# Attention block and gated MLP in one kernel: softmax scaling and weight split moved to ScalarE, local probabilities transposed by DMA from batch 2, block sums added from PSUM on VectorE

## The chip, the cores and the metric

The kernel runs on one core of a Trainium2 chip. The metric is the time of one execution on the device in microseconds (us). Engines are named as in the profile: PE is TensorE, DVE is VectorE, ACT is ScalarE, POOL is GpSimd, SP is the engine that issues the DMAs.

## The reference

q, k and v are 8 batches x 8 heads x 576 positions x 64. Each head runs two attentions and adds them: one over positions averaged in groups of 4 (144 of them), repeated back to 576, and one over a band of seven neighbours. The 4608 x 512 result goes through a gated MLP.

```python
q_d = q.reshape(B, H, Sd, factor, D).mean(axis=3)      # k_d, v_d alike; factor 4
out_up = np.repeat(sm_attn(q_d, k_d, v_d), factor, axis=2)
mask = np.abs(pos[:, None] - pos[None, :]) < factor
scores = np.where(mask, scale * np.matmul(q, k.transpose(0, 1, 3, 2)), -1000000000.0)
attn = np.exp(scores - np.max(scores, axis=-1, keepdims=True))
attn = attn / (np.sum(attn, axis=-1, keepdims=True) + 1e-09)
attn_out = out_up + np.matmul(attn, v)
x = attn_out.transpose(0, 2, 1, 3).reshape(B * S, H * D)
return (1.0 / (1.0 + np.exp(-(x @ w_gate)))) * (x @ w_val) @ w_out
```

## The kernel before

A unit is one pair of heads of one batch: 32 units, four a batch, unit u belongs to batch u // 4. For each unit the local attention works on 10 blocks of 58 queries against 64 keys, two heads on two halves of the partitions. Its steps are s0 and s1 (scores, tile `s`, 40 products of 64x64; scaled and masked into `t`, 128 x 640), then maximum, subtraction and exp on `t`, step sm (sum, reciprocal, multiplication), steps a0 and a1 (`t_local`: five 128x128 transposes by PE into PSUM, tile `at`, and the split of the result into two float16 parts), and step x (`av_local`: 30 products into tile `x`, to which DVE adds the pooled result `od`; then the split of the sum for the MLP). The pooled attention has the steps prep2 and vd (sums of 4 on POOL), d0 and d1 (products `sd`, exp with accumulated sums), dn (normalised into `ad`), at (`adt`, transposes by PE) and od.

float32 operands of the MLP are carried as two float16 parts (hi and lo) and multiplied with three products. The weights of gate (g) and value (v) are rebuilt from 64-bit words in batch 0 (`wjoin`), scaled by a power of two and split (`wsplit`, lines 280 to 296): DVE, ACT or POOL scales in place, ACT casts hi, POOL subtracts for lo.

Batches 0 and 1 run the MLP plainly: gate and value products (`pg`, `pv`), tanh on ACT, `act_val` on DVE, then the output products `po`. During batch 1, `sums` builds combinations of weight blocks and stores them to DRAM (`wd`). Batches 2 to 7 use seven products in place of eight for each pair of blocks (function `pair`, lines 804 to 873): six matmuls a product, and the seven results are added up by s1, s6, s7, s2, s5, s3 and s4 from five PSUM buffers (pool `ps_m`) into SBUF.

The work of the units of batch b + 1 is strewn over the MLP of batch b. The table `T` gives every step a position; all steps are sorted by it and emitted, and a scheduler then fixes one order of instructions on each engine, which each engine keeps at run time. An engine that waits for a semaphore holds up all that stands behind it in its order. SP issues every DMA in one such order.

Of the kernel before, what the change touches and what calls it, by code (L numbers as in the profile page):

```python
# [64 lines left out]
def attention_moe(ctx, tc, qk, qkd, v, vd, wg, wv, wo, mask, out):  # L65
# [214 lines left out]
    def wsplit(k, i):  # L280
# [126 lines left out]
    def sum4(out, x, eng=nc.gpsimd):  # L407

        nc.gpsimd.tensor_tensor(out=x[:, :, 0:2], in0=x[:, :, 0:2], in1=x[:, :, 2:4], op=ALU.add)  # L409
        for ps, o, g in out:  # L410
            eng.tensor_tensor(out=o, in0=x[ps, g, 0], in1=x[ps, g, 1], op=ALU.add)
# [24 lines left out]
    def unit_steps(u):  # L436
# [3 lines left out]
        plain = u < NPLAIN  # L440
# [27 lines left out]
        def prep2():  # L468
# [4 lines left out]
            sum4([(ALL, s["qd"], slice(0, SD))] + [(ps, s["kd"][ps, h], slice(SD, 2 * SD)) for h, ps in enumerate(HALVES)], x)  # L473

        def s_products(groups):
# [9 lines left out]
            if u < NPAIR:  # L485
# [602 lines left out]
```

## Time and profile before

| | us |
|---|---|
| median of 3 runs | 1049.86 (1049.4 to 1056.17) |
| the profiled execution | 1052.21 |
| its span, first to last instruction | 1050.4 |

| engine | busy us | share of the span |
|---|---|---|
| PE | 1017.0 | 97% |
| DVE | 752.5 | 72% |
| POOL | 537.2 | 51% |
| ACT | 475.0 | 45% |

The busy time of an engine is that of its instructions; of PE the ends are modelled, so that it reads as nearly full also where it waits a little. A share over the whole span hides that the stages have different limits: the start (weights and batch 0, up to about 175 us), batch 1 (to about 350 us), five alike batches of some 119 us, and the last batch, which has no attention beside it. The granted clock of PE is 1.00 in nearly every slice after 325 us.

### The profile page before, as it was taken

How to read it: one execution, taken by the hardware profiler on the slowest of the kernel's cores; microseconds unless marked ns; L12 is line 12 of the kernel's file. 1: busy time of each engine (PE TensorE's matmuls, PEld its weight loads, DVE VectorE, ACT ScalarE, POOL GpSimd, SP SyncE). 2: the span in 40 equal slices, each digit the busy share in tenths (PEclk: the TensorE clock that was granted, in tenths of full speed). 3: DMA queues.
4: the chain of work that ended last, by engine and by line, in shares of the span. 5: the costliest groups of instructions: out<-in, count | busy, mean ns of one | idle time of the engine just before them, and what ended most of it. 6: DMA issues, size and time to landing. Idle time of an engine off the chain costs nothing.

```text
span 1050.4 us, 23772 instructions
## 1 busy us (share of the span) xinstructions
PE 1017.0 (97%) x9587; PEld 813.0 (77%) x9587; DVE 752.5 (72%) x1417; ACT 475.0 (45%) x1064; POOL 537.2 (51%) x579
## 2 busy tenths in 40 slices
PE   8997989998989999999999999999999999999998
PEld 6875768876767887787778887787778887887776
DVE  6989989478796788747886479747886479825640
ACT  4868756334443444434443344524544344522320
POOL 7435378442554648545673548545573557512320
PEclk9999998999998999999999999999999999999999
DMA  9458943332434356344553356344563355313501
GB/s 366 158 177 254 352 146 130 130 123 99 145 141 152 127 202 228 118 148 164 200 206 117 127 197 251 122 147 141 192 234 102 132 190 192 117 35 119 179 31 46
DMA packets 53245, 169.01 MB, mean 161 GB/s; under 512 B 12560, under 2 KB 18832, under 8 KB 53136
## 3 DMA queue, kind: packets, MB, share of 16 engines
q1 hardware_dynamic: 53136, 167.50, 46.0%
q8 instruction: 75, 1.23, 0.5%
q14 instruction: 34, 0.28, 0.1%
HBM read 147.03 MB, written 20.45 MB: 159 GB/s over the span
## 4 chain that ended last, share of the span: by engine, by line
PE 65%; DVE 17%; ACT 6%; issue 5%; DMA 4%; POOL 2%; SPq 0%; DVEq 0%; POOLq 0%; ACTq 0%
PE po L420 27%; PE pv L420 14%; PE pg L420 14%; PE x L420 2%; PE s L483 2%; DVE vblk L192 2%; DVE tanh L719 2%; DVE arena L828 2%; PE sd L420 2%; PE od L420 2%; DMA v<-in_v_dram 1%; DMA wd<-arena 1%; ACT gq L865 1%; DVE arena L784 1%; PE at L580 1%
## 5 line engine op out<-in xcount | busy, mean ns | idle before, releaser
L420 PEld LDWEIGHTS <-arena 128*128 128x128 f16 x4176 | 407.0, 98 | 130.0 <-issue 16.1
L420 PE MATMUL po<-gq,wo 128*128 128x288 f16 x2304 | 295.2, 288 | 3.2 <-ACT gq L191 3.2
L420 PE MATMUL pg<-arena 128*128 128x288 f16 x2088 | 278.3, 287 | 6.1 <-DVE tanh L719 2.4
L420 PE MATMUL pv<-arena 128*128 128x288 f16 x2088 | 278.3, 288 | 6.0 <-DVE arena L828 2.7
L420 PEld LDWEIGHTS <-wo 128*128 128x128 f16 x2304 | 225.5, 98 | 61.5 <-issue 3.7
L828 POOL TENSOR_TENSOR arena<-arena 128x288 f32<-128x288 f32 x126 | 121.8, 971 | 122.7 <-ACT arena L842 92.2
L828 DVE TENSOR_TENSOR arena<-pv,arena 128x288 f32<-128x288 f32 x180 | 78.3, 447 | 50.4 <-PE pv L420 32.2
L746 DVE TENSOR_SCALAR arena<-po,osc 128x288 f32<-128x288 f32 x32 | 16.5, 515 | 82.9 <-PE po L420 82.8
L192 DVE SCALAR_TENSOR_TENSOR vblk<-v,svb,vblk 64x640 f16<-64x640 f32 x52 | 66.2, 1273 | 6.4 <-ACT vblk L191 4.4
L191 ACT ACTIVATE vblk<-v,svb 64x640 f16<-64x640 f32 x52 | 42.9, 825 | 44.5 <-PE x L420 24.9
L828 DVE TENSOR_TENSOR arena<-pg,arena 128x288 f32<-128x288 f32 x126 | 54.8, 449 | 5.0 <-PE pg L420 3.0
L514 POOL TENSOR_TENSOR t<-t,mx 128x640 f32<-128x640 f32 x32 | 44.3, 1384 | 26.6 <-DVE mx L513 15.2
L565 POOL TENSOR_TENSOR ad<-e,sme 72x288 f32<-72x288 f32 x54 | 42.1, 797 | 22.0 <-DVE sme L556 13.3
L524 POOL TENSOR_TENSOR t<-t,sm 128x640 f32<-128x640 f32 x24 | 35.5, 1479 | 29.2 <-DVE sm L522 21.1
L409 POOL TENSOR_TENSOR qkd<-qkd 128x576 f32<-128x576 f32 x29 | 36.7, 1265 | 26.1 <-DMA qkd<-in_qkd_dram 25.9
L548 ACT ACTIVATE e<-sd,mxd 72x144 f32<-72x144 f32 x128 | 47.0, 371 | 1.9 <-POOL ad L565 0.4
L409 POOL TENSOR_TENSOR vd<-vd 128x384 f32<-128x384 f32 x29 | 25.0, 862 | 43.5 <-DMA vd<-in_vd_dram 42.9
L420 PE MATMUL sd<-kdblk,qks 128*72 128x288 f32 x128 | 42.8, 416 | 3.8 <-ACT e L548 2.6
L775 POOL TENSOR_TENSOR arena<-arena 128x1024 f32<-128x1024 f16 x12 | 26.6, 2214 | 38.9 <-DMA wd<-arena 34.2
L295 POOL TENSOR_TENSOR arena<-arena 128x512 f16<-128x512 f32 x24 | 33.1, 1395 | 25.4 <-ACT arena L294 25.2
L483 PE MATMUL s<-qk 64*64 64x64 f32 x1200 | 43.3, 224 | 0.0
L483 PEld LDWEIGHTS s<-qk 64*64 64x64 f32 x1200 | 38.6, 137 | 6.0 <-issue 3.9
(147 smaller groups left out, 1543.8 us busy)
## 6 DMA issues: line engine op xcount, KB each, us to landing
arena<-wd SPq DMA_DIRECT2D x72, 896.0 KB, 4.6
qk<-in_qk_dram SPq DMA_DIRECT2D x30, 610.0 KB, 5.1
qkd<-in_qkd_dram SPq DMA_DIRECT2D x29, 576.0 KB, 3.9
vd<-in_vd_dram SPq DMA_DIRECT2D x29, 384.0 KB, 4.1
v<-in_v_dram SPq DMA_DIRECT2D x32, 320.0 KB, 4.5
arena<-in_wg_dram SPq DMA_DIRECT2D x12, 512.0 KB, 4.3
arena<-in_wv_dram SPq DMA_DIRECT2D x12, 512.0 KB, 4.5
arena<-in_wo_dram SPq DMA_DIRECT2D x12, 512.0 KB, 5.9
```

The lines of the kernel that those rows point to most:

```text
L191: nc.scalar.activation(hi, src, AF.Copy, scale=sc)
L192: return nc.vector.scalar_tensor_tensor(out=lo, in0=src, scalar=sc, in1=hi, op0=ALU.mult, op1=ALU.subtract)
L295: nc.gpsimd.tensor_tensor(out=lo, in0=a, in1=hi, op=ALU.subtract)
L409: nc.gpsimd.tensor_tensor(out=x[:, :, 0:2], in0=x[:, :, 0:2], in1=x[:, :, 2:4], op=ALU.add)
L420: nc.tensor.matmul(o, w[a], x[c], start=first and i == 0, stop=last and i == len(pairs) - 1)
L483: return nc.tensor.matmul(o, qkraw[u][ps, g * R : g * R + WIN], kw[ps, g], start=True, stop=True)
L514: nc.gpsimd.tensor_tensor(out=t, in0=t, in1=mx.unsqueeze(2).to_broadcast([P, NBLK, WIN]), op=ALU.subtract)
L524: eng.tensor_tensor(out=t, in0=t, in1=sm.unsqueeze(2).to_broadcast([P, NBLK, WIN]), op=ALU.mult)
L548: nc.scalar.activation(s["e"][:, qb, h, :], pt[:QM, h * SD : (h + 1) * SD], AF.Exp, bias=mx[:, h : h + 1], scale=QKSCALE / 16, accum_out=s ...
L565: eng.tensor_tensor(out=AD[:, qb].rearrange("p c h k -> p h c k")[:, :, :, :KC], in0=s["e"][:, qb].rearrange("p h (c k) -> p h c k", c=NKC ...
L775: whole = nc.gpsimd.tensor_tensor(out=x.rearrange("p (f c) -> p f c", f=2), in0=home[k][:, 2 * p : 2 * p + 2, 0], in1=home[k][:, 2 * p : 2 ...
L828: eng.tensor_tensor(out=dst_, in0=x, in1=y, op=ALU.add)
```

## The change

Six edits, each behind a switch in `T`:

- Local softmax (`eb`): scores are formed with the opposite sign, the row minimum takes the place of the maximum, and exp runs on ACT as ten instructions of 128x64, each with its block's bias. The subtraction on POOL is gone. Step sm (`nb`): the multiplication by the reciprocal, which POOL did for 24 units and DVE for 8, becomes ten instructions of 128x64 on ACT. The small addition of EPS moves from DVE to ACT for both softmaxes (`tz`).
- Pooled softmax (`ae=1`): from unit 8 on the normalisation into `ad` is four ACT instructions in place of two on POOL.
- Weight split (`ws`): ACT scales and casts hi in one instruction, DVE forms lo; the scaling in place and the subtraction on POOL are gone.
- `dt=8`: for units 8 to 31 (batches 2 to 7) `t` is split into two float16 parts in SBUF (tile `hl`, one buffer), and one DMA on SP transposes both into `at16` (one buffer). The PE transposes and the reading of their PSUM tile are gone for these units. Steps a0 and a1 are put behind step x of the unit before.
- Block sums (`wa=3`): in s7, DVE adds the product from PSUM directly, without the ACT copy and the POOL addition; in s5, DVE reads the product twice, and the POOL addition is gone.
- `sr=8`: the two groups of score products of batch 1's units are issued separately again.

`pr`, `pw` and `acs` are 0 and `da` is 99, so the code behind them (sums of 4 by DVE, pooled transposes by DMA) is not used. `m0a0` and `m1a0` in `T` change their positions.

```diff
-T = dict(ax0=0, ax1=0, ax2=1,
+T = dict(pr=0, pw=0, ae=1, dt=8, da=99, sr=8, eb=1, nb=1, tz=1, ws=1, wa=3, acs=0, ax0=0,
...
         if k == "o":
+            split(hi, lo, a, sc)
+        elif T.get(f"ws{WORDER.index((k, i))}", T["ws"]):
             split(hi, lo, a, sc)
...
+    def shift(a, plus, times, on_act):
+        if on_act:
+            nc.scalar.activation(a, a, AF.Copy, bias=plus * times, scale=times)
...
-                scalar=QKSCALE, in1=mk[:, j0:j1, :], op0=ALU.mult, op1=ALU.add)
+                scalar=-QKSCALE if fl("eb", u) else QKSCALE, in1=mk[:, j0:j1, :], op0=ALU.mult, op1=ALU.subtract if fl("eb", u) else ALU.add)
...
+            if fl("eb", u):
+                nc.vector.tensor_reduce(mx, t, axis=AX.X, op=ALU.min)
...
+                for g in range(NBLK):
+                    nc.scalar.activation(t[:, g], t[:, g], AF.Exp, bias=mx[:, g : g + 1], scale=-1.0, **(dict(accum_out=s["sm"][:, g : g + 1]) if fl("acs", u) else {}))
+                return
...
-            nc.vector.tensor_scalar(out=sm, in0=sm, scalar1=EPS, scalar2=1.0 if plain else 2.0 ** -10, op0=ALU.add, op1=ALU.mult)
+            shift(sm, EPS, 1.0 if plain else 2.0 ** -10, fl("tz", u))
             nc.vector.reciprocal(sm, sm)
+            if fl("nb", u):
+                for g in range(NBLK):
+                    nc.scalar.activation(t[:, g], t[:, g], AF.Copy, scale=sm[:, g : g + 1])
+                return
...
         def t_local(j0, j1):
+            if j0 == 0:
+                s["at16"] = wk.tile([P, 2, NBLK, WIN], F16, tag="hl" if not swap and u % 2 else "at", name=f"at16_{u}", bufs=1)
+                s["at"] = in_parts(s["at16"], NBLK)
+            if swap:
+                if j0 == 0:
+                    t = s["t"].rearrange("p j c -> p (j c)")
+                    hl = wk.tile([P, 2, NJ * 2 * WIN], F16, tag="hl", name=f"hl_{u}", bufs=1)
+                    parts_of([hl[:, 0], hl[:, 1]], t)
+                    nc.sync.dma_start_transpose(s["at16"].rearrange("p t a b -> p (t a b)").rearrange("p (j r) -> p j r", r=P), hl.rearrange("p t c -> p (t c)"))
+                return
...
         def s7():
+            if T["wa"] & 1:
+                plus(sx[:, 3], go(P7), sx[:, 1])
+                return
...
-            plus(sx[:, 0], go(P5), sx[:, 1])
-            plus(j["c"][:, 3], sx[:, 0], sx[:, 2], nc.gpsimd)
+            pt = go(P5)
+            plus(sx[:, 0], pt, sx[:, 1])
+            if T["wa"] & 2:
+                plus(j["c"][:, 3], pt, sx[:, 3])
...
     def at(u, k):
+        p = placed(u, k)
+        return max(p, placed(u - 1, "x") + (0.05 if k == "a0" else 0.1)) if k in ("a0", "a1") and u >= T["dt"] else p
```

The order on ACT at the start of the program, before: `t_185` is unit 0's local softmax, `mxd` and `e` its pooled one, `wo_110` borrowed room for v.

```order
L462 COPY wo_110<-v_152 64x10x64 x2
L546 ACTIVATE mxd_0_228<-mxd_0_228 72x2
L548 ACTIVATE e_226,sme_227<-sd_0_224,mxd_0_228 72x144 x2
L546 ACTIVATE mxd_1_239<-mxd_1_239 72x2
L515 ACTIVATE t_185<-t_185 128x640
L548 ACTIVATE e_226,sme_227<-sd_1_237,mxd_1_239 72x144 x2
L561 ACTIVATE ad<-e_226,sme_227 72x3x48 x4
```

The same place after the change:

```order
L481 COPY wo_110<-v_152 64x10x64 x2
L537 ACTIVATE t_185<-t_185,mx_205 128x64 x10
L587 ACTIVATE mxd_0_236<-mxd_0_236 72x2
L587 ACTIVATE mxd_1_247<-mxd_1_247 72x2
L589 ACTIVATE e_234,sme_235<-sd_0_232,mxd_0_236 72x144 x2
L589 ACTIVATE e_234,sme_235<-sd_1_245,mxd_1_247 72x144 x2
L431 ACTIVATE sm_284<-sm_284 128x10
L431 ACTIVATE sme_235<-sme_235 72x4
L554 ACTIVATE t_185<-t_185,sm_284 128x64 x10
L610 ACTIVATE ad<-e_234,sme_235 72x3x48 x4
```

One exp has become ten, ten multiplications and two small additions have come in; each of units 0 to 3 gets as many before the first tanh of batch 0.

DVE in the last gate and value blocks of the last batch, before: the sums of `pg` and, behind them, of `pv`; the second number in `pg_5_44` says which of the seven products it is.

```order
L828 TENSOR_TENSOR arena<-pg_5_44_13192,arena 128x288
L828 TENSOR_TENSOR arena<-pg_5_11_13209,arena 128x288
L870 SCALAR_TENSOR_TENSOR gq<-tanh,gq 128x2x576
L828 TENSOR_TENSOR arena<-pg_5_33_13217,arena 128x288
L828 TENSOR_TENSOR arena<-pg_5_62_13226,arena 128x288
L828 TENSOR_TENSOR arena<-pg_5_26_13234,arena 128x288
```

And after the change:

```order
L893 TENSOR_TENSOR arena<-pg_5_44_13522,arena 128x288
L893 TENSOR_TENSOR arena<-pg_5_55_13530,arena 128x288
L893 TENSOR_TENSOR arena<-pg_5_11_13538,arena 128x288
L942 SCALAR_TENSOR_TENSOR gq<-tanh,gq 128x2x576
L893 TENSOR_TENSOR arena<-pg_5_33_13546,arena 128x288 x2
L893 TENSOR_TENSOR arena<-pg_5_62_13555,arena 128x288
L893 TENSOR_TENSOR arena<-pg_5_26_13563,arena 128x288
```

DVE has seven additions a block where it had five; product 55 was copied by ACT before, product 33 is read twice now.

ACT after the change in the middle of batch 4, behind step x of unit 20 (the two `vblk` casts wait for it): `hl_9082` is unit 22's, `t_8628` unit 22's, `t_8911` unit 23's, `od_21` unit 21's.

```order
L196 ACTIVATE vblk<-v_7767,svb 64x10x64 x2
L693 CAST arena<-xs 128x288
L621 COPY adt_21_8833<-adt_8826 128x432
L554 ACTIVATE t_8628<-t_8628,sm_8711 128x64 x10
L431 ACTIVATE sme_8663<-sme_8663 72x4
L901 COPY arena<-pg_3_00_8552 128x288
L621 CAST hl_9082<-t_8628 128x640
L537 ACTIVATE t_8911<-t_8911,mx_8914 128x64 x10
L610 ACTIVATE ad<-e_8662,sme_8663 72x3x48 x4
L937 ACTIVATE gq<-tanh 128x2x576
```

Nothing of unit 21's transposition stands here: it is on SP, and the cast into `hl` for unit 22 writes the buffer which that DMA reads. DVE's part of it stands behind the addition of pg_3_44:

```order
L893 TENSOR_TENSOR arena<-pg_3_44_8562,arena 128x288
L623 TENSOR_TENSOR hl_9082<-t_8628,hl_9082 128x640
L192 TENSOR_REDUCE vm_9490<-v_9389 128x1
L893 TENSOR_TENSOR arena<-pg_3_11_8585,arena 128x288
L192 TENSOR_REDUCE vm_9490<-v_9428 128x1
L893 TENSOR_TENSOR arena<-pg_3_55_8577,arena 128x288
```

On PE, between step x of unit 20 and the copied product pg_3_00 stand five products of pv_2, the 40 score products of unit 23 and pg_3_00 itself; between the x steps of units 21 and 22 stand six products, unit 24's scores and 90 matmuls `po`.

## Rows read from the trace of the kernel before

**Rows 1.** The page, part 1: busy us, share of the span, instructions.

```profile
PE 1017.0 (97%) x9587; PEld 813.0 (77%) x9587; DVE 752.5 (72%) x1417; ACT 475.0 (45%) x1064; POOL 537.2 (51%) x579
```

**Rows 2.** Windows by stage: busy us and instructions by engine, clock, DMA.

```profile
210.00:315.00 105.00, 95.63 (x901) 74.90 (x900) 85.92 (x150) 46.31 (x104) 49.74 (x43) 0.96 0.36 127
...
597.70:716.80 119.10, 118.30 (x1162) 95.19 (x1160) 84.62 (x161) 51.35 (x115) 66.10 (x76) 1.00 0.49 169
```

**Rows 3.** Chain that ended last, in order of time: start, us, what; last batch.

```profile
949.85 5.14 PE pg L420 x42
```

**Rows 4.** Timeline of PE, 640 to 672 us: start, us, operation.

```profile
640.68 0.38 PE L580 MATMUL at<-ident,t 128*128 128x128 f32 x2
640.90 0.65 PE L420 MATMUL sd<-kdblk,qks 128*72 128x288 f32 x2
...
651.69 1.38 PE L483 MATMUL s<-qk 64*64 64x64 f32 x40
653.00 2.38 PE L420 MATMUL pv<-arena 128*128 128x288 f16 x18
```

**Rows 5.** Window 9.56 to 65.36 us, first ACT instruction to first tanh; columns as rows 2.

```profile
9.56:65.36 55.80, 51.29 (x504) 42.50 (x503) 50.44 (x110) 41.35 (x111) 36.08 (x42) 1.00 0.61 222
```

**Rows 6.** Timeline of ACT, 8 to 80 us.

```profile
17.43 1.33 ACT L561 ACTIVATE ad<-e,sme 72x144 f32<-72x144 f32 x4 [0.96 <-DVE sme L556]
```

**Rows 7.** ACT groups by line and shape: busy us, mean ns | idle before.

```profile
L191 ACT ACTIVATE vblk<-v,svb 64x640 f16<-64x640 f32 x52 | 42.9, 825 | 44.5 <-PE x L420 24.9 <-DVE svb L184 18.9
...
L515 ACT ACTIVATE t<-t 128x640 f32<-128x640 f32 x32 | 23.5, 734 | 11.1 <-POOL t L514 10.2
...
L561 ACT ACTIVATE ad<-e,sme 72x144 f32<-72x144 f32 x16 | 5.4, 405 | 1.0 <-DVE sme L556 1.0
...
L546 ACT ACTIVATE mxd<-mxd 72x2 f32<-72x2 f32 x64 | 12.8, 199 | 21.4 <-DVE mxd L545 21.2
```

**Rows 8.** DVE and POOL groups by line and shape.

```profile
L828 DVE TENSOR_TENSOR arena<-pv,arena 128x288 f32<-128x288 f32 x180 | 78.3, 447 | 50.4 <-PE pv L420 32.2 <-PE sd L420 8.3 <-ACT arena L836 7.1
...
L514 POOL TENSOR_TENSOR t<-t,mx 128x640 f32<-128x640 f32 x32 | 44.3, 1384 | 26.6 <-DVE mx L513 15.2 <-DVE ew L174 7.0 <-DVE mxg L166 4.1
...
L565 POOL TENSOR_TENSOR ad<-e,sme 72x288 f32<-72x288 f32 x54 | 42.1, 797 | 22.0 <-DVE sme L556 13.3 <-DVE eo L174 3.7 <-ACT arena L241 2.3
...
L295 POOL TENSOR_TENSOR arena<-arena 128x512 f16<-128x512 f32 x24 | 33.1, 1395 | 25.4 <-ACT arena L294 25.2
...
L192 DVE SCALAR_TENSOR_TENSOR wo<-wo,co 128x512 f16<-128x512 f32 x12 | 9.8, 831 | 0.2 <-ACT wo L191 0.2
...
L293 DVE TENSOR_SCALAR arena<-arena,cw 128x512 f32<-128x512 f32 x19 | 11.1, 637 | 0.0
```

**Rows 9.** Line 192 on DVE over the program: min/median/max ns of one.

```profile
L192 DVE SCALAR_TENSOR_TENSOR vblk<-v,svb,vblk x52: 868/952/3879, 180.1 to 925.4; 64x640 f16<-64x640 f32 x52
```

**Rows 10.** DVE groups in 210 to 316 us.

```profile
L784 DVE TENSOR_TENSOR arena<-arena 128x256 f32<-128x256 f32 x34 | 19.2, 598 | 7.4 <-POOL arena L775 7.2
L192 DVE SCALAR_TENSOR_TENSOR vblk<-v,svb,vblk 64x640 f16<-64x640 f32 x6 | 12.6, 2104 | 0.1
L788 DVE TENSOR_TENSOR arena<-arena 128x1024 f16<-128x1024 f32 x9 | 11.0, 1224 | 4.6 <-ACT arena L787 4.6
```

**Rows 11.** Timeline of PE, 210 to 320 us: instructions that waited.

```profile
251.56 2.02 PE L420 MATMUL pg<-arena 128*128 128x288 f16 x12 [2.36 <-DVE tanh L719]
```

**Rows 12.** Timeline of PE, 400 to 960 us: first and last of eight that waited.

```profile
402.49 3.83 PE L420 MATMUL pv<-arena 128*128 128x288 f16 x30 [0.24 <-DVE arena L828]
...
644.31 1.63 PE L420 MATMUL pv<-arena 128*128 128x288 f16 x12 [0.28 <-DVE arena L828]
```

**Rows 13.** DMA issues: count, KB each, median us from issue to landing.

```profile
v<-in_v_dram SPq DMA_DIRECT2D x32, 320.0 KB, 4.5
...
gq<-in_vd_dram SPq DMA_DIRECT2D x3, 384.0 KB, 10.8
...
out_dram<-arena SPq DMA_DIRECT2D x8, 32.0 KB, 1.7
```

More of the change, by code (lines that the diff above doesn't have):

```diff
@@ L405, in pairs_done, with sum4, fl @@
         return b < 2 or (b, 2 * NP - 1) in seen
[L407 removed]
+    def sum4(out, x, reduce=False):
+        if reduce:
+            for ps, o, g in out:
+                nc.vector.tensor_reduce(o, x[ps, g], axis=AX.X, op=ALU.add)
+            return
         nc.gpsimd.tensor_tensor(out=x[:, :, 0:2], in0=x[:, :, 0:2], in1=x[:, :, 2:4], op=ALU.add)
         for ps, o, g in out:
[L411 removed]
+            nc.gpsimd.tensor_tensor(out=o, in0=x[ps, g, 0], in1=x[ps, g, 1], op=ALU.add)
     ALL = slice(0, P)
     HALVES = [slice(0, 64), slice(64, P)]
+    def fl(k, u):
+        return T.get(f"{k}{u}", T[k])
+    def shift(a, plus, times, on_act):
+        if on_act:
+            nc.scalar.activation(a, a, AF.Copy, bias=plus * times, scale=times)
+        else:
+            nc.vector.tensor_scalar(out=a, in0=a, scalar1=plus, scalar2=times, op0=ALU.add, op1=ALU.mult)
     def product(o, w, x, first=True, last=True):
@@ L495, in s_local @@
             n = j1 - j0
-            if u < NPAIR:
+            if not srun:
                 s_products([(j0, j1)])
@@ L552, in norm_down @@
         def norm_down():
-            own(ad, u)
+            if u == T["da"]:
+                zero(adw)
+            own(adw, u)
             sme = s["sme"]
-            nc.vector.tensor_scalar(out=sme, in0=sme, scalar1=EPS, scalar2=4.0, op0=ALU.add, op1=ALU.mult)
+            shift(sme, EPS, 4.0 * (2.0 ** -10 if dswap else 1.0), fl("tz", u))
             nc.vector.reciprocal(sme, sme)
-            eng = nc.vector if T.get(f"ae{u}", 0) == 2 else nc.gpsimd
+            if dswap:
+                e = s["e"].rearrange("p q h c -> p (q h) c")
+                nc.gpsimd.tensor_tensor(out=e, in0=e, in1=sme.unsqueeze(2).to_broadcast([QM, 4, SD]), op=ALU.mult)
+                for qb in range(2):
+                    parts_of([ad16[:QM, i, qb].rearrange("p c h k -> p h c k")[:, :, :, :KC] for i in range(2)], s["e"][:, qb].rearrange("p h (c k) -> p h c k", c=NKC))
+                return
+            eng = nc.vector if T.get(f"ae{u}", T["ae"]) == 2 else nc.gpsimd
             for qb in range(2):
-                if T.get(f"ae{u}", 0) == 1:
+                if T.get(f"ae{u}", T["ae"]) == 1:
                     for h in range(2):
@@ L598, in av_down @@
             for c in range(NKC):
-                product(pt[:, :SD], [VDB[:, c]], [s["adt"][:, c]], c == 0, c == NKC - 1)
+                if dswap:
+                    product(pt[:, :SD].rearrange("p (q r) -> p q r", q=2), [vd16[u % 2][:, i, c] for i in range(2)],
+                            [s["adt"][:, i, :, c, :QM] for i in range(2)], c == 0, c == NKC - 1)
+                else:
+                    product(pt[:, :SD], [VDB[:, c]], [s["adt"][:, c]], c == 0, c == NKC - 1)
             od = wk.tile([P, SD], F32, tag="od", name=f"od16_{u}")
-            if u < NPAIR:
+            if u < NPAIR or dswap:
                 nc.scalar.copy(od, pt[:, :SD])
@@ L610, in av_local @@
             for i in range(i0, i1):
-                product(pt[:, (i - i0) * R : (i - i0 + 1) * R], [x[:, i] for x in VBp], [x[:, i] for x in s["at"]])
+                product(pt[:, (i - i0) * R : (i - i0 + 1) * R], [x[:, i] for x in VBp], [x[:, i, :R] for x in s["at"]])
             if i0 == 0:
```

52 lines of the change are left out of this document (38 added, 14 removed).

## The prediction

> **What bounds the kernel now.** I read the page's busy shares first: PE is busy 97% of the span, no other engine above 72% [rows 1]. Busy PE can be waiting PE, so the windows by stage come next. In a middle batch PE is idle for 119.1 - 118.3 = 0.8 us, at full clock, while DVE is at 71% and ACT at 43% [rows 2]. That this is real work is seen in the chain of waits in the last batch: 42 matmuls of 288 columns follow one another in 5.14 us, 0.122 us each [rows 3], so a product of six takes 0.735 us. In the middle batches only eight instructions waited, about a quarter of a microsecond each [rows 12]. There, time goes only with work that leaves PE, and comes with whatever makes PE wait.
>
> Two stages are different. In batch 1's gate and value phase PE is idle 105.0 - 95.6 = 9.4 us and its clock averages 0.96; one wait there, for DVE's tanh product, is 2.36 us [rows 2, 11]. At the start, from ACT's first instruction to the first tanh, DVE is busy 50.4 of 55.8 us and ACT 41.35 [rows 5]: DVE bounds it, and ACT has 14.4 us to spare. The profiled execution took 1052.21 us, 2.3 above the median of 1049.86. I make the sum as differences and put them on the median.
>
> **PE transposes.** Two of them stand between two other operations at 640.68 and 640.90 us: 0.22 us for two, 0.11 each, although each record lasts longer [rows 4]. A unit has five, 0.55 us. Of the 24 units from unit 8, 20 (12 to 31) lie in the five PE-bound batches: 20 x 0.55 = **-11.0 us**. The other four units, 2.2 us, fall into batch 1's stage. In exchange ACT casts and DVE subtracts 640 columns in SBUF instead of 580 from PSUM: no difference on either engine that I count.
>
> **ACT's new work.** Four instructions of 144 columns with a scale per partition took 1.33 us, one 405 ns: they start (1.33 - 0.405) / 3 = 0.308 us apart [rows 6, 7]. Between 2 and 640 columns the price rises by (734 - 199) / 638 = 0.84 ns a column [rows 7], so one of 64 costs 0.308 - 80 x 0.00084 = 0.241 us and ten 2.41. A unit gets twenty (4.82), loses one exp (0.73), and gets two small additions of 0.2 each [rows 7]: +4.5 us; from unit 8 also four for the pooled normalisation, +1.3. In a middle batch ACT goes up by 4 x 5.8 = 23 us less twelve copies of s7, which leaves it below 65%: beside PE's work, not on its path.
>
> At the start it isn't beside. Before the first tanh stand all of units 0 to 3: 4 x 4.5 = 18 us, and eight weight casts now carry a scale, 825 against 734 ns at 640 columns [rows 7], +0.7. ACT's 41.35 us become 60.0, and the stretch was 55.8 [rows 5]. Were ACT never idle, the first tanh would be 4.3 us late; were it idle as DVE, the busiest engine before, was (busy 90%), 60.0 / 0.904 = 66.4, 10.6 us late; if nothing of the added work found an idle place, 18.7. I take 7.5, between the first two, **+7.5 us**: the third would need idle ACT time to stay as it is, though DVE gets lighter there by the multiplications and small additions.
>
> **Weight split.** The latency of a piece falls: a POOL subtraction of 1.395 us goes, DVE has 0.83 (lo, as for `wo`) instead of 0.637 (scaling) [rows 8]. That is at most 24 x 0.83 - 19 x 0.637 = 7.8 us more on DVE over all 24 pieces, against the multiplications and EPS additions of the eight units there, which are about as much. Counted as nothing; the cover is DVE's own relief, and if that is gone the 7.8 come on top.
>
> **Batch 1.** DVE's subtraction for `vblk` has a minimum of 868 ns over the program but a mean of 2104 ns in this stage [rows 9, 10]; `sums` additions of 256 columns take 598 ns, while additions of 288 columns with an operand in PSUM take 447 [rows 8, 10]. Both kinds read and write SBUF alone, and I put their excess down to POOL working beside them: 6 x 1.24 + 34 x 0.15 = 12.5 us. POOL loses four subtractions, about two multiplications of the same size and about six pooled normalisations: 6 x 1.384 + 6 x 0.797 = 13.1 of 49.7 us [rows 2, 8], 26%. So DVE regains 0.26 x 12.5 = 3.3 us, and PE loses 2.2 us of transposes: **-5.5 us**. It can be nothing or a loss: ACT's ten-packs stand before the `sums` cast for which DVE waited 4.6 us [rows 10]; if that doubles, the 5.5 shrink to about one. At most the stage gives up all idle time and all lost clock, 9.4 + 0.04 x 105 + 2.2 = 15.8 us.
>
> **Block sums.** A block costs DVE two more additions of 0.447 us [rows 8]: 24 a batch, 10.7 us, on 84.6 of 119.1 [rows 2]: 80%, less the EPS additions. ACT's copy and POOL's additions go. PE has five buffers of 0.735 us; a queue on DVE of more than some 3 us makes it wait. It waited eight times so far [rows 12]; I add 0.4 us a batch, **+2 us**. Nothing would be kind, and one such wait of 0.24 in each of a batch's twelve blocks makes 5 x 12 x 0.24 = 14 us.
>
> Sum: -11.0 + 7.5 - 5.5 + 2 = **-7 us, 1043 us**. Own range 1035 to 1051. About 1% (10.5 us; below 1039.4, above 1060.4) is what a measurement of this kernel tells from no change.
>
> **The DMA transposition.** No row shows one. It moves 320 KB. The nearest row by size and engine queue is the load of v, 320 KB, 4.5 us from issue to landing; the ends are 1.7 us (smallest store) and 10.8 (loads queued at the start) [rows 13]. I take 4.5. It starts when step x of the unit before has left PE (one `at16` buffer), and the earliest that needs it is not its own step x but the next unit's cast into `hl`, whose one buffer it reads. In the middle of a batch that cast stands behind pg_3_00, which ends six products and 40 score products after x: 6 x 0.735 + 1.31 = 5.7 us [rows 3, 4]. At 4.5 us nobody waits. Behind the DMA on SP stand loads into a ring of three buffers, each wanted two blocks later.
>
> **Rivals.**
>
> *The transposition lands late, and the kernel is slower.* Then ACT stands at the cast, DVE at the subtraction behind it, and neither empties PE's buffers. PE can still fill five after pg_3_44, until 5.7 + 6 x 0.735 = 10.1 us after x; the first buffer is free again after landing plus the cast (0.73), two DVE operations of 640 columns (0.87 each) and an addition (0.45), 2.9 us [rows 7 to 9]. It decides from a landing of 7.2 us on. At 10.8 PE loses 3.6 us at one unit in each of five batches, 18 us: -7 + 18 = +11, 1061 us; the gain is eaten from 8.6 us on. For it: DMA was busy half the time in these batches [rows 2]. Against: every median of a like size is below 6 us. 19%. The Trainium skill speaks for this rival in "VectorE: DVE Perf Modes", section "The three transpose paths": 390 ns for a 128x128 block on TensorE against 1309 ns by DMA, and the advice to use TensorE where PSUM will do; ten blocks one after another would be an estimated 13.1 us, 1072 us by the same sum. The Trainium skill's page "Advanced Engine Details and Errata", section "X-Bar Transpose (TRN2)", says that such DMAs are as fast as others, which would leave the sum as it is. No run here shows either yet; the row of PE has 110 ns a block, not 390.
>
> *The whole of batch 1's loss goes, and DVE's relief hides ACT's burden but for its floor:* -11.0 - 15.8 + 4.3 = -22.5, **1027 us**. For it: 2.1 us against 0.87 for one operation [rows 9, 10], and POOL loses 24 weight subtractions too. Against: the `sums` chain itself (POOL, DVE, ACT, store) stays. 28%.
>
> *ACT bounds the start altogether:* -11.0 - 5.5 + 18.7 + 2 = +4, **1054 us**. For it: ACT's order is fixed, and every ten-pack stands before weight work. Against: 14.4 us of idle ACT time. 13%.
>
> That the transposes stay on PE is excluded by the order: units 8 to 31 have none. The forecast keeps 40%.
>
> **Range and chances.** Low 1024 lies just under the second rival, high 1066 takes in late landings up to 11.8 us; beyond lie most of 14 us on DVE and the page's 13.1 us. Faster: all 28 of the second rival and 18 of the forecast's 40, 0.46. Same: 22 of the forecast, 10 of ACT's case, 3 of the late landing, 0.35. Slower: 16 + 3, 0.19.
>
> **What would show it.** In the profile after: a middle batch of about 117 us with PE idle below 1.5 us; a first tanh at 73 us; batch 1's phase about 5 us shorter; the group of ten-packs near 240 ns a start; the DMA transposition landing in 4 to 6 us; `vblk` on DVE near 950 ns. Wrong would be: PE waiting for DVE in the middle of each batch, with ACT before it waiting for a DMA; a first tanh beyond 80 us; middle batches that lost less than 1 us.

## The result, and the profile after

The changed kernel takes 1041.32 us (median; 1039.38 to 1041.78) against 1052.34 for the kernel before on the same chip: a ratio of 0.991, interval 0.9883 to 0.9938. The profiled execution took 1041.09 us, 11.1 less than the one of before. The forecast was 1043 us, 7 below before; on the same chip the change gave 11.0. The sum came out within the range; several of its terms did not.

The page, part 1, after (busy us, share, instructions), answers to [rows 1]:

```profile
PE 999.2 (96%) x9467; PEld 796.3 (77%) x9467; DVE 742.4 (71%) x1470; ACT 613.7 (59%) x1733; POOL 238.2 (23%) x305
```

POOL's busy time fell by more than half, ACT's rose by 139 us. PE lost 120 instructions, the transposes of 24 units. Windows by stage after (columns as [rows 2]): up to the first tanh, batch 1's gate phase, batch 2's, an alike batch.

```profile
9.56:76.69 67.13, 57.65 (x504) 46.73 (x503) 43.82 (x103) 57.91 (x195) 16.10 (x27) 0.87 0.52 187
...
223.90:311.36 87.46, 84.33 (x805) 66.54 (x804) 64.52 (x119) 63.87 (x192) 33.27 (x29) 1.00 0.40 127
...
354.11:442.12 88.01, 80.37 (x789) 63.06 (x788) 76.56 (x154) 63.87 (x197) 20.51 (x24) 0.98 0.59 187
...
595.44:710.84 115.40, 114.98 (x1140) 92.58 (x1139) 88.04 (x173) 69.23 (x198) 25.13 (x36) 1.00 0.58 187
```

The first tanh comes at 76.69 us, 11.3 late, with ACT busy 57.9 of 67.1 us and DVE now only 43.8 [rows 5]. The alike batch is 3.7 us shorter [rows 2], though DVE is busier in it. Batch 2's gate phase has 7.6 us of idle PE.

To compare kernels I cut each profiled execution at the first gate product of each batch. The last batch and what follows, 100.7 us, is the same in all of them to 0.1 us but for e6 (101.2). Columns in us; a ratio is to runs of the kernel before on the same chip:

| kernel | to batch 0 | batch 0 | 1 and 2 | 3 to 6 | median | ratio to before |
|---|---|---|---|---|---|---|
| before | 60.0 | 152.1 | 263.4 | 474.3 | 1049.86 | |
| after | 72.3 | 151.6 | 256.1 | 458.6 | 1041.32 | 0.991 (0.9883 to 0.9938) |
| e1 transposes on PE | 72.6 | 146.7 | 255.8 | 465.6 | 1044.61 | 0.995 (0.9929 to 0.9972) |
| e2 start as before | 60.8 | 151.6 | 257.2 | 457.7 | 1029.14 | 0.9788 (0.9749 to 0.9827) |
| e3 sums as before | 74.9 | 150.0 | 255.0 | 470.1 | 1053.94 | 1.0029 (1.0006 to 1.0051) |
| e4 split as before | 71.8 | 149.4 | 255.0 | 458.0 | 1038.04 | 0.9871 (0.9848 to 0.9894) |
| e5 sums alone | 60.1 | 152.7 | 263.4 | 473.3 | 1048.58 | 0.9988 (0.996 to 1.0015) |
| e6 s5 alone | 60.0 | 150.4 | 262.3 | 471.3 | 1047.2 | 0.9973 (0.995 to 0.9995) |
| e7 transposition alone | 59.4 | 157.6 | 267.2 | 476.4 | 1058.03 | 1.0066 (1.004 to 1.0093) |
| e8 e2 and e4 | 60.3 | 151.5 | 255.7 | 457.8 | 1027.88 | 0.9783 (0.976 to 0.9806) |
| e9 softmax alone | 70.7 | 151.5 | 257.1 | 469.2 | 1053.84 | 1.0035 (1.001 to 1.0061) |
| e10 e8, units 12 to 15 by PE | 61.9 | 150.1 | 254.0 | 462.5 | 1033.48 | 0.9819 (0.9785 to 0.9853) |
| e11 e8, units 4 to 7 back | 62.3 | 152.7 | 255.9 | 457.9 | 1031.1 | 0.9779 (0.9744 to 0.9813) |
| e12 sums and exp | 60.7 | 151.9 | 261.0 | 466.8 | 1042.17 | 0.9911 (0.9884 to 0.9938) |

Batch 0 differs by 4.9 us between after and e1, whose orders on ACT and DVE are the same there, so a few us in that column alone mean nothing; where they come from was not traced. The columns behind it repeat better: 457.7 to 458.6 in the five kernels with all edits from batch 3 on. A profiled execution need not lie at the median: e7's took 1063.08 us, 5 above it, e5's 1051.98, 3.4 above.

### The profile page after: what moved, and what is told of

Read it like the earlier page. It is cut to its first block, busy times and chain, and to the rows that moved or that the text cites. A ratio compares the mean times of both kernels' runs of the same rounds, so it can differ in the third digit from the quotient of the medians.

```text
span 1039.3 us, 23856 instructions
## 1 busy us (share of the span) xinstructions
PE 999.2 (96%) x9467; PEld 796.3 (77%) x9467; DVE 742.4 (71%) x1470; ACT 613.7 (59%) x1733; POOL 238.2 (23%) x305
## 2 busy tenths in 40 slices
DMA packets 84736, 176.89 MB, mean 170 GB/s; under 512 B 44048, under 2 KB 50320, under 8 KB 84624
## 4 chain that ended last, share of the span: by engine, by line
PE 71%; DVE 9%; DMA 5%; ACT 4%; POOL 2%; issue 2%; SPq 0%; ACTq 0%; DVEq 0%; POOLq 0%
PE po L439 23%; PE pv L439 20%; PE pg L439 19%; PE s L502 3%; PE x L439 2%; PE sd L439 2%; PE od L439 2%; DVE arena L849 1%; DMA v<-in_v_dram 1%; DVE vblk L197 1%; DMA arena<-in_wv_dram 1%; DMA arena<-in_wo_dram 1%; PE adt L651 1%; DVE arena L893 1%; POOL arena L840 1%
## 5 line engine op out<-in xcount | busy, mean ns | idle before, releaser
L893 DVE TENSOR_TENSOR arena<-pv,arena 128x288 f32<-128x288 f32 x252 | 107.0, 452 | 33.6 <-PE pv L439 27.4
L537 ACT ACTIVATE t<-t,mx 128x64 f32<-128x64 f32 x320 | 80.0, 336 | 28.4 <-DVE mx L533 28.3
L554 ACT ACTIVATE t<-t,sm 128x64 f32<-128x64 f32 x320 | 80.4, 337 | 12.5 <-DVE sm L551 12.3
L893 DVE TENSOR_TENSOR arena<-pg,arena 128x288 f32<-128x288 f32 x180 | 77.4, 449 | 10.2 <-PE pg L439 7.4
L811 DVE TENSOR_SCALAR arena<-po,osc 128x288 f32<-128x288 f32 x32 | 16.4, 513 | 75.0 <-PE po L439 74.9
L901 ACT COPY arena<-pg 128x288 f32<-128x288 f32 x36 | 14.1, 392 | 74.8 <-PE pg L439 74.8
L813 ACT ACTIVATE arena<-po,osc 128x288 f32<-128x288 f32 x32 | 15.2, 496 | 64.8 <-PE po L439 64.8
L196 ACT ACTIVATE vblk<-v,svb 64x640 f16<-64x640 f32 x52 | 42.8, 823 | 11.6 <-PE x L439 10.7
L693 ACT CAST arena<-arena 128x576 f16<-128x576 f32 (+1 forms) x24 | 21.9, 911 | 41.7 <-DVE arena L689 28.5
L421 POOL TENSOR_TENSOR qks<-qkd 128x144 f32<-128x144 f32 x29 | 14.3, 492 | 138.0 <-PE sd L439 137.0
L714 POOL TENSOR_TENSOR arena<-arena 128x288 f32<-128x288 f32 x12 | 9.5, 796 | 152.1 <-DVE arena L689 152.0
L610 ACT ACTIVATE ad<-e,sme 72x144 f32<-72x144 f32 x112 | 37.4, 403 | 11.2 <-DVE sme L599 11.2
```

The source lines that it names most:

```text
L196: nc.scalar.activation(hi, src, AF.Copy, scale=sc)
L537: nc.scalar.activation(t[:, g], t[:, g], AF.Exp, bias=mx[:, g : g + 1], scale=-1.0, **(dict(accum_out=s["sm"][:, g : g + 1]) if fl("acs", ...
L554: nc.scalar.activation(t[:, g], t[:, g], AF.Copy, scale=sm[:, g : g + 1])
L610: nc.scalar.activation(AD[:, qb, :, h, :KC], s["e"][:, qb, h].rearrange("p (c k) -> p c k", c=NKC), AF.Copy, scale=sme[:, 2 * qb + h : 2 * ...
L693: nc.scalar.copy(dst_[:, :, 0], src)
L811: nc.vector.tensor_scalar(out=dst_, in0=pt[:, :HN], scalar1=sc, scalar2=None, op0=ALU.mult)
```

## The experiments

**e1.**

```diff
-dt=8
+dt=99
```

> The changed kernel with the transposes of units 8 to 31 put back on PE; everything else of the change stays. My theory: the alike batches lost 3.65 us each (119.0 to 115.4) because a transpose costs PE more than the 0.11 us I took (3.65 / 20 = 0.18), and the block sums cost nothing. Then the alike batches return to 118.5 to 119.5 us and, with batch 2's wait behind the late transposition (2.0 us) gone again, the whole is 1041 + 4 x 3.65 + 3 - 2 = about 1057 us, slower than before. Rival: part of the 3.65 us comes from the lighter POOL and the sums read straight from PSUM; then a batch gets back only the predicted 2.2 us, 117.6 us each, and the whole is 1041 + 5 x 2.2 - 2 = 1050 us. If the transposition by DMA gave nothing: 1041 us or below.

Neither: 1044.6 us, between after and before; its interval just overlaps that of after. An alike batch, in a window:

```profile
592.05:709.01 116.96, 116.96 (x1160) 94.84 (x1159) 87.51 (x177) 69.65 (x203) 26.81 (x36) 1.00 0.51 173
```

PE has no idle time, and as many matmuls as before the change, in 117.0 us where it took 119.1 [rows 2]. So the 119.1 held 2.1 us of waits, of which only 0.8 showed as idle; the rest stood under modelled ends. From e1 to after, busy PE falls by 117.0 - 115.0 = 2.0 us for 20 transposes, 0.10 each; 0.4 comes back as waits. Over batches 3 to 6 the transposition by DMA gives 7.0 us, over 1 and 2 nothing: it pays here, where sums and softmax are off POOL; e7 has it without both, e3 without the sums.

**e2.** The ten-packs of units 0 to 3 undone:

```diff
+eb0=0, eb1=0, eb2=0, eb3=0, nb0=0, nb1=0, nb2=0, nb3=0
```

> The changed kernel, with the local softmax of units 0 to 3 alone as before: one exp of 640 columns on ACT behind POOL's subtraction, and POOL's or DVE's multiplication in place of ten instructions on ACT; all other units keep the ten-packs. My theory: ACT bounds the start, since it is busy 57.9 of the 67.1 us up to the first tanh and the ten-packs of four units are 20.0 us of that. Then the first tanh comes back from 76.7 us to 66 to 68 us (65.4 before the change), batch 1's gate phase starts 8 to 11 us earlier and the whole is 1030 to 1033 us. Rival: the weight split that now needs ACT and DVE in turn holds the start; then the first tanh stays beyond 73 us and the whole at 1037 us or above. A second rival: the earlier start is given back by the end of batch 0, where weights are waited for; then the first tanh is early but the whole is 1038 us or above.

My theory, and a little better. The window up to the first tanh:

```profile
9.56:65.11 55.55, 50.91 (x500) 42.42 (x501) 49.22 (x104) 41.77 (x118) 27.21 (x31) 1.00 0.61 224
```

ACT is back at 41.8 us busy and the tanh at 65.1; the other columns of the table stay.

**e3.**

```diff
-wa=3
+wa=0
```

> The changed kernel with the block sums as before: s7's product copied by ACT and added by POOL, one addition of s5 on POOL; DVE has 24 additions a batch fewer. My theory: with 88 us of 115.4 DVE still empties PE's buffers in time, PE is idle only 0.4 us in an alike batch, so these stay at 115.0 to 116.0 us; in batch 2, where PE waited 1.4 us for DVE's sums and 2.0 for an ACT copy, up to 2 us go either way. The whole: 1039 to 1043 us. Rival (as I predicted): DVE's additions cost 0.4 us a batch or more; then the whole is 1037 us or below. Rival: the sums straight from PSUM are what took 0.8 us of idle PE out of each alike batch; then these return to 116 to 117 us and the whole is 1045 us or above.

The second rival, and more: batches 3 to 6 get 11.5 us longer, and all of the change's gain is gone. The timeline of e3, POOL, ACT and PE in batch 4 (start, us, instruction, [wait and releaser]):

```profile
634.27 0.83 POOL L419 TENSOR_TENSOR vd<-vd 128x384 f32<-128x384 f32 x1 [1.89 <-DMA vd<-in_vd_dram]
635.05 0.79 POOL L893 TENSOR_TENSOR tanh<-arena 128x288 f32<-128x288 f32 x1
...
635.88 1.25 ACT L781 ACTIVATE tanh<-tanh,tsc 128x1152 f32<-128x1152 f32 x1 [2.02 <-POOL tanh L893]
637.04 0.38 ACT L901 COPY arena<-pv 128x288 f32<-128x288 f32 x1
...
637.47 0.90 PE L439 MATMUL pv<-arena 128*128 128x288 f16 x6 [2.81 <-ACT arena L901]
```

Read upwards: PE waits 2.81 us for a buffer that ACT's copy empties; the copy stands in ACT's order behind a tanh; the tanh waits for POOL's addition; that stood in POOL's order behind a sum of 4 which waited for a load.

**e4.**

```diff
-ws=1
+ws=0
```

> The changed kernel with the weight split as before: a scaling in place on DVE, ACT or POOL, the cast on ACT, the subtraction for lo on POOL. My theory: batch 0's gate and value phase got 4.0 us shorter (103.5 to 99.6) because this subtraction and POOL's other work left it; with POOL otherwise nearly empty now, most of the gain stays without this edit: the phase is 100 to 103 us and the whole 1041 to 1044 us. Rival: the split is what shortens that phase and DVE's slow operations beside POOL come back; then the whole is 1045 us or above. Rival: ACT's scaled cast is a burden at the start, where ACT is the bound; then the first tanh comes 1 to 2 us earlier and the whole is 1039 us or below.

The time of the last rival, 1038.0 us, some 3 less than after, but not its sign: the tanh comes at 76.15, only 0.5 earlier, and the rest lies in batch 0 and its neighbours, where 2 us are no evidence. The interval overlaps that of after; that the split costs something is likely, not shown.

**e5.** The kernel before, all switches but the sums off:

```diff
-eb=1, nb=1, tz=1, ws=1, ae=1, dt=8, wa=3
+eb=0, nb=0, tz=0, ws=0, ae=0, dt=99, wa=3
```

> The kernel before with the block sums alone: s7's product and both additions of s5 by DVE from PSUM; softmax, weight split and transposes as before. My theory: in the batches before, ACT's tanh waited for a POOL addition (4.3 us in one batch), the copy of s7 stood behind it on ACT, DVE's sums behind the copy and PE behind DVE; these waits cost 2.1 us a batch, since the same batch without a wait takes 116.9 us. Without the POOL addition and the copy the alike batches take 116.9 to 117.3 us and the whole 1050.6 - 4 x 2.1 - about 1 = about 1041 us. Rival: the sums on DVE pay only beside an ACT that is full of ten-packs; then the alike batches stay at 118.5 to 119 us and the whole is 1048 to 1051 us. As I predicted (0.4 us more a batch): 1052 us.

The rival's time (1048.6), though not its reason. Timeline of e5 in batch 4:

```profile
642.05 1.98 POOL L421 TENSOR_TENSOR kdblk<-qkd 64x144 f32<-64x144 f32 x2
644.11 1.26 POOL L540 TENSOR_TENSOR t<-t,mx 128x640 f32<-128x640 f32 x1
...
645.40 0.74 ACT L541 ACTIVATE t<-t 128x640 f32<-128x640 f32 x1 [3.84 <-POOL t L540]
646.48 0.38 ACT L901 COPY arena<-pv 128x288 f32<-128x288 f32 x1
...
646.91 2.37 PE L439 MATMUL pv<-arena 128*128 128x288 f16 x18 [1.51 <-ACT arena L901]
```

The same chain with another head: ACT's exp waits for POOL's subtraction, the copy of a product behind it comes late, PE waits. With the sums gone from POOL and ACT, this wait takes the place of the tanh's. What ACT waited for in batches 3 to 6, before and in e5 (us in total, times, longest):

```profile
ACT tanh L716 <- POOL tanh L828: 15.2, 4, 4.3
...
ACT t L541 <- POOL t L540: 37.6, 14, 4.2
```

Before, the exp waited 1.9 us there in all.

**e6.** As e5, with `wa=2`.

> The kernel before with one of the two edits of the block sums alone: in s5 DVE reads the product twice and the POOL addition into the tanh's input is gone; s7 keeps its ACT copy and its POOL addition. My theory: it is the tanh that waits for POOL which holds ACT's order up, so most of the gain is here: alike batches of 117.2 to 118 us and the whole 1043 to 1046 us. Rival: the copy of s7 on ACT is what DVE waits for (3.5 us in one batch), however ACT got late; then the batches stay at 118.5 us or more and the whole is 1048 us or above.

Between the two: 1047.2 us. Batches 3 to 6 lose 3.0 us, but e5, which has this edit too, loses 1.0 there, so that 2 us are within the spread and the share of the tanh's wait is not shown. The exp's wait stayed.

**e7.** As e5, with `dt=8` and `wa=0`.

> The kernel before with the transposition by DMA alone (units 8 to 31, with the later places of a0 and a1); softmax, split and block sums as before. By my prediction's terms: 24 x 0.55 = 13.2 us less, 1037.5 us. My theory after the first experiments: the alike batches lose 1.6 to 2.2 us each, batches 1 and 2 together nothing, since one landing there took 9.8 us: 1043 to 1046 us. Rival: the waits of ACT at the cast behind a DMA that is not yet through eat all of it, with the copy of s7 behind that cast: 1048 us or above.

The rival's side, and beyond it: 8 us slower than before. The view of tile `hl` (idle time before its instructions, us and times, by releaser):

```profile
  POOL t L557: 11.6, 5
  DMA at<-hl: 7.9, 9
```

Alone, the edit puts a cast on ACT that waits for POOL's multiplication, 11.6 us over five times, and 7.9 for the DMA. With ten-packs the multiplication is on ACT itself and the first wait can't arise. But over batches 3 to 6 it loses only 2.1 us in the profiled execution, which is one of the long ones; 5.5 of the rest lie in batch 0, which I can't explain.

**e8.** e2 and e4 together.

> The changed kernel with both losses taken out: the local softmax of units 0 to 3 as before and the weight split as before. Theory: the two gains (12 and 3 us) add up, 1025 to 1027 us. Rival: the split cost 3 us only because ACT bound the start; with the start relieved DVE's slow operations beside POOL come back and the whole is 1029 us or above.

1027.9 us, just between the two; e2 and e8 can't be told apart. Either beats both kernels: about 22 us below before.

**e9.** As e5, with `eb=1, nb=1, tz=1, ae=1, wa=0`.

> The kernel before with the two softmax edits alone (ten-packs and the EPS additions on ACT, the pooled normalisation on ACT); weight split, transposes by PE and block sums as before. My theory: this edit makes the loss at the start and the gain of batch 1, since it takes the most work from POOL: first tanh at 75 to 77 us (65.4 before), batches 1 and 2 together 255 to 258 us (263.4), and the alike batches stay at 118 to 119 us, because ACT's copy of s7 now stands behind ten-packs: 1050 + 11 - 7 - 2 = about 1052 us. Rival: the softmax on ACT alone frees the alike batches from POOL too; then they take 117 us and the whole is 1043 to 1046 us. Rival: batch 1's gain comes from the weight split; then batches 1 and 2 stay at 262 us or more and the whole is 1058 us or above.

My theory in each stage, with a whole of 1053.8 us: tanh at 75.1, batches 1 and 2 at 257.1, an alike batch at 118.3:

```profile
596.52:714.77 118.25, 117.73 (x1161) 94.69 (x1160) 81.09 (x148) 72.67 (x215) 51.46 (x60) 1.00 0.49 171
```

Batch 1 takes 132.8 us here, 143.0 before and 130.2 after: its gain belongs to the softmax, not to the weight split.

**e10.** e8, and units 12 to 15 excepted from `swap` and from the later places of a0 and a1:

```diff
+u >= T["dt"] and not 12 <= u < 16
```

> The version with the softmax of units 0 to 3 and the weight split as before (1027.9 us), and with the transposes of units 12 to 15, which are prepared in batch 2, back on PE at their places of before; all other units from 8 on keep the transposition by DMA. Theory: batch 2's gate phase has about 7 us of waits (one behind a landing of 9.8 us); without these four transpositions batch 2 takes 122 to 124 us in place of 126.4, in spite of 2.2 us more work on PE, and the whole is 1024 to 1026 us. Rival: batch 2's waits come from the block combinations that batch 1 left over, as in the run with all transposes on PE, where batches 1 and 2 together took 255.8 us against 256.1; then nothing is gained: 1027 to 1031 us.

Worse. Batch 2 gets its 2.3 us (124.1 for 126.4), but batch 3 takes 119.7 in place of 114.8, with one new wait. The timeline of PE, and the window behind the wait (columns as [rows 2]):

```profile
508.79 3.04 PE L439 MATMUL pv<-arena 128*128 128x288 f16 x12 [2.83 <-DVE xs L689]
...
508.79:511.80 3.01, 3.01 (x13) 1.93 (x13) 3.01 (x8) 0.88 (x3) 1.81 (x3) 0.50 0.36 76
```

PE waits 2.83 us, and for the next 3.0 us its granted clock is 0.50, the lower of its two levels, so that the wait costs about half as much again (3.0 x 0.5 = 1.5 us): 4.3 of the 4.9.

**e11.** e8, and `eb4` to `eb7`, `nb4` to `nb7` at 0.

> The same version with the local softmax of units 4 to 7 as before too, so that batch 0 has no ten-packs at all. Theory: in batch 0's gate phase and output products ACT is still the engine that weights and units wait for; those stages, 100.0 and 51.6 us, come to 98 and 48.5 us as before the change, and the whole is 1022 to 1025 us. Rival: these units' POOL instructions bring the slow operations of DVE back; the gain is eaten in the same stages or in batch 1, and the whole is 1027 to 1032 us.

The rival: no gain, in batch 0 either (152.7 us against 151.5). DVE's operations on SBUF are longer there than in e8, as it says: the scaling of a weight piece 771 ns in place of 511, the product into `gq` 1073 in place of 960.

**e12.** As e5, with exp as ten-packs for units 8 to 31:

```diff
+eb=1, eb0=0, eb1=0, eb2=0, eb3=0, eb4=0, eb5=0, eb6=0, eb7=0
```

> The kernel before with the block sums by DVE, and, for units 8 to 31 alone, exp as ten instructions on ACT without POOL's subtraction; the multiplication by the reciprocal stays on POOL, everything else as before, batch 0 untouched. My theory: with the block sums alone ACT's exp waited 3.8 us for POOL's subtraction, ACT's copy of a product stood behind it and PE waited 1.5 us for that copy; each edit alone leaves one wait for POOL in ACT's order, and the gain comes when both are gone. Then the alike batches take 116.9 to 117.4 us (118.8 with the sums alone, 118.3 with the softmax alone), the start stays as before (first tanh at 65 to 66 us) and the whole is 1039 to 1043 us. Rival: the multiplication on POOL still loads POOL so that its sums of 4 and DVE's operations beside it hold the batches at 118 us or more; then the whole is 1046 us or above. Rival: the ten-packs on an ACT with other work behind them cost what they give: 1048 us or above.

My theory. From batch 3 on neither the local exp nor tanh nor a copy waits for POOL now (1.1 us is left at the pooled exp, 9.1 at the split of the sum), and an alike batch:

```profile
590.97:708.42 117.45, 117.29 (x1161) 94.78 (x1160) 88.90 (x185) 53.87 (x138) 37.51 (x48) 1.00 0.49 172
```

These two edits alone make as much as the whole change, without its loss at the start.

## Why the prediction was right in the sum and wrong in its terms

By stages the forecast was: start +7.5, batches 1 and 2 together -5.5 - 2.2 + 0.4 = -7.3, batches 3 to 6 4 x (-2.2 + 0.4) = -7.2. Measured: up to batch 1's first product +11.9 (223.9 against 212.0), -7.3, and -15.7. Two misses of opposite sign met, and the middle sum is right only because batch 1 gained more than forecast and batch 2 lost. That the whole came this near is luck.

*The start was mis-sized.* ACT's floor was right: 60.0 us forecast, 57.9 measured, and so were the ten-packs:

```profile
L537 ACT ACTIVATE t<-t,mx 128x64 f32<-128x64 f32 x320 | 80.0, 336 | 28.4 <-DVE mx L533 28.3
L554 ACT ACTIVATE t<-t,sm 128x64 f32<-128x64 f32 x320 | 80.4, 337 | 12.5 <-DVE sm L551 12.3
```

(groups of after: busy us, mean ns | idle before). 80.0 / 320 = 0.250 us a start, where I had 0.241. The step that failed is the value taken between the bounds: a tanh 7.5 us late left ACT 3.3 us of idle time in 63.3. It had 9.2 in 67.1, of which 7.0 lie behind 67.4 us, where the last unit's chain of PE, ACT and DVE runs to the first tanh and ACT has nothing else to do. The middle bound, ACT as busy as DVE had been (10.6), was close; e2 shows that these eighty instructions make it.

*The block sums had the wrong sign.* I counted DVE's added instructions and took PE's waits as 0.8 us a batch, of which nothing could be won. The waits were 2.1 us (e1). One way to them leads from POOL through ACT, and I had not followed the waits [rows 12] further than to DVE (from 400 to 960 us they are twelve; the timeline that I counted eight in ended at 666 us). The timeline of before:

```profile
655.77 0.79 POOL L828 TENSOR_TENSOR tanh<-arena 128x288 f32<-128x288 f32 x1
656.59 1.25 ACT L716 ACTIVATE tanh<-tanh,tsc 128x1152 f32<-128x1152 f32 x1 [4.27 <-POOL tanh L828]
657.75 0.38 ACT L836 COPY arena<-pv 128x288 f32<-128x288 f32 x1
658.17 1.38 DVE L828 TENSOR_TENSOR arena<-pv,arena 128x288 f32<-128x288 f32 x3 [1.83 <-ACT arena L836]
```

Tanh waits for POOL, the copy for the tanh, DVE for the copy. PE's next product starts at 658.18, right behind the copy, though PE shows no wait there. The recorded waits of PE in batches 3 to 6 of before are all for DVE, and DVE was also held up by its own operations: the product with tanh was longer than in e12, where POOL works 37.5 us a batch in place of 66.1 [rows 2]. Waits of PE in before (us, times, longest), then this operation in before and in e12, batches 3 to 6:

```profile
PE pv L420 <- DVE arena L828: 2.2, 8, 0.4
PE pg L420 <- DVE arena L828: 0.4, 1, 0.4
...
L719 DVE SCALAR_TENSOR_TENSOR tanh<-tanh,arena 128x1152 f32<-128x1152 f32 x12 | 22.4, 1863 | 1.2
...
L784 DVE SCALAR_TENSOR_TENSOR tanh<-tanh,arena 128x1152 f32<-128x1152 f32 x12 | 16.2, 1354 | 0.1
```

The way through ACT is recorded up to PE in e3 and e5. How much of before's 2.1 us came that way, and how much through DVE's longer operations, no run separates: what empties POOL takes both away.

In the changed kernel the sums are worth 11.5 us in batches 3 to 6 (e3); alone, 1.0 (e5); together with the exp, 7.5 (e12). The softmax alone gives 5.1 (e9), the transposition alone loses 2.1 (e7) and beside the softmax without the sums gains nothing (470.1 us in e3, 469.2 in e9). Added up, the three alone are 4.0 us; together they gave 15.7. So edits that I added up one by one depend on each other: in e3 and e5 ACT's order still hangs on POOL, once by the sums, once by the softmax.

*The PE transposes* cost 0.10 us each (forecast 0.11): right, 2.0 us a batch. Of the -11.0 us, 7.0 came, in batches 3 to 6; that batches 1 and 2 give nothing, and that the rest needs the other edits (e7), I had not forecast.

*Batch 1* gained 12.8 us (143.0 to 130.2), near the rival that took the whole loss. The window that I had read [rows 2] holds 7.5 us of the output products. Gate phase and output products of batch 1 before, then the output products after:

```profile
212.00:307.50 95.50, 89.13 (x820) 69.85 (x820) 77.36 (x136) 41.73 (x97) 48.11 (x41) 0.96 0.35 123
307.50:355.10 47.60, 44.41 (x416) 35.07 (x415) 33.68 (x51) 17.21 (x31) 22.55 (x22) 0.93 0.42 148
...
311.40:354.10 42.70, 40.86 (x410) 33.25 (x409) 26.12 (x46) 14.55 (x31) 17.05 (x18) 1.00 0.60 199
```

The gate phase lost 8.0 us: its clock rose from 0.96 to 1.00, PE's idle time fell from 6.4 to 3.1 us. The output products lost 4.8, which I had not forecast; their clock rose from 0.93 to 1.00. `vblk` on DVE came down from 2104 ns [rows 10] to

```profile
L197 DVE SCALAR_TENSOR_TENSOR vblk<-v,svb,vblk 64x640 f16<-64x640 f32 x6 | 6.7, 1121 | 2.3 <-ACT vblk L196 2.2
```

e9 puts the gain down to the softmax. But batch 2 gave 5.6 us back, which no term of mine held. Two of its waits, 1.3 and 2.5 us, come at its start and are for DVE's operations at the end of batch 1's output, among the last block combinations; in the 3.1 us behind them the clock is 0.53 (columns as [rows 2]):

```profile
354.10:361.70 7.60, 3.76 (x27) 2.61 (x26) 6.00 (x10) 5.86 (x20) 1.92 (x2) 1.00 0.00 0
361.70:364.80 3.10, 3.08 (x13) 1.89 (x13) 2.74 (x8) 3.07 (x14) 0.00 (x0) 0.53 0.87 303
```

Other runs have waits at the same place (e9 2.0 us, e1 2.7, e12 4.9, before none). In e1 their chain reads:

```profile
348.35 2.13 POOL L840 TENSOR_TENSOR arena<-arena 128x1024 f32<-128x1024 f16 x1 [4.93 <-DMA wd<-arena]
350.51 3.33 DVE L849 TENSOR_TENSOR arena<-arena 128x256 f32<-128x256 f32 x4 [1.13 <-POOL arena L840]
...
354.87 1.15 ACT L693 CAST arena<-arena 128x1152 f16<-128x1152 f32 x1
...
356.07 0.28 PE L439 MATMUL pg<-arena 128*128 128x288 f16 x1 [2.70 <-ACT arena L693]
```

POOL waits for a store of `sums`; DVE's part of that block combination comes late; ACT casts the combination (from 353.92) and only behind it, in its order, batch 2's input (L693). Batch 1 got shorter than its chain of combinations. A third wait of batch 2 is the rival of the late transposition, in one place. Timeline of after, SP, ACT and PE:

```profile
394.48 0.33 SPq L210 DMA_DIRECT2D vd<-in_vd_dram  x1
394.86 0.43 SPq L210 DMA_DIRECT2D qk<-in_qk_dram  x1
395.39 0.37 SPq L210 DMA_DIRECT2D qkd<-in_qkd_dram  x1
395.85 0.38 SPq L864 DMA_DIRECT2D arena<-wd  x1
396.32 0.38 SPq L210 DMA_DIRECT2D v<-in_v_dram  x1
396.92 4.92 SPq L634 DMA_TRANSPOSE at<-hl  x1
...
406.80 0.72 ACT L621 CAST hl<-t 128x640 f16<-128x640 f32 x1 [2.75 <-DMA at<-hl]
...
407.87 1.63 PE L439 MATMUL pg<-arena 128*128 128x288 f16 x12 [2.04 <-ACT arena L901]
```

Five loads are issued in the 2.5 us ahead of it; ACT stands at the cast into `hl`, as forecast, and PE waits 2.04 us. The mechanism and its place were right; ACT waited for it at this cast seven times, 6.7 us in all, but it decided once in 24, not once a batch. All 24 of after:

```profile
L634 SPq DMA_TRANSPOSE at<-hl x24: 1259/1352/4919, 242.1 to 913.7; - x24
...
DMA to landing us min/median/max: 3.3/3.8/9.8
```

The median of 3.8 us lies by my 4.5. The Trainium skill's "Advanced Engine Details and Errata", section "X-Bar Transpose (TRN2)", where such DMAs are as fast as others, agrees with that: a load of 320 KB took 4.9 in the same run. The 1309 ns a block in the Trainium skill's "VectorE: DVE Perf Modes", section "The three transpose paths", would have made an estimated 13.1 us for ten; none of the 24 took as long, and the median is under a third of it.

*The weight split*, counted as nothing, may cost up to 3 us beside ACT's ten-packs (e4, not shown) and nothing that can be told without them at the start (e8 against e2).

Open: how much of batch 2's length (120.3 us before; 123.0 in e1 to 127.4 in e2, 126.2 in e7 with the softmax as before) each of these waits makes, and what lies behind e7's long batch 0. Spreading the five loads ahead of the late transposition wasn't tried.

## What to carry to other kernels

Follow a small wait of the bounding engine back through every engine's order to its head, not only to the first releaser: one slow engine at the head of an in-order queue sets all that stands behind it, and edits that free such a queue can pay far more together than alone (here 15.7 us against 4.0), so price them as a set. A stage that is bound by another engine wants the opposite edit: the ten-packs that freed the alike batches cost 12 us at the start, where undoing them for four units gave the best kernels here. Where ends are modelled, take the waits of a stage as its length less that of the same work without waits, not as its idle time.

## What was not expected of the hardware

A transposition holds the SP queue for 1.35 us in the median and 4.92 at most, where each load ahead of the late one took 0.33 to 0.43 and no load or store of that run more than 1.40. With it the page counts 44048 packets under 512 bytes against 12560 before and in e1: 31488 / 24 = 1312 for one transposition of 320 KB.
